# Feature sums of batch 0: from a masked sum on VectorE to a masked operand on GpSimd and small matmuls on TensorE

## The chip, the cores and the metric

The kernel runs on one core of a Trainium2 chip, in one launch. The metric is the time on the device in microseconds (us). A core has engines that run their own queues in order and wait for one another by semaphores: TensorE (PE in the profile, its weight loads PEld), VectorE (DVE), ScalarE (ACT), GpSimd (POOL) and SyncE (SP, which here issues most of the transfers).

## What is computed

The reference has two parts. The first is attention with a sketched polynomial kernel, without softmax: 4 batches, 4 heads, 1088 positions, 32 dimensions a head, r = 8, so 64 features.

```python
def phi(x):
    a = einsum('rd,bhsd->bhsr', S1, x)
    b = einsum('rd,bhsd->bhsr', S2, x)
    return einsum('bhsi,bhsj->bhsij', a, b)      # reshaped to r*r = 64 features
q_p, k_p = phi(q), phi(k)
kv = einsum('bhsf,bhsd->bhfd', k_p, v)
z = sum(k_p, axis=2)                             # feature sums, over all positions
num = einsum('bhsf,bhfd->bhsd', q_p, kv)
den = einsum('bhsf,bhf->bhs', q_p, z)[..., None] + 1e-06
attn = num / den
```

The second part is a gated feed-forward layer over the 4352 tokens, 128 wide: `sigmoid(x @ w_gate) * (x @ w_val) @ w_out` with 1536 inner columns. The weights and S1, S2 arrive as 64-bit floats and are narrowed to 32 bits on the chip; everything is computed in 32-bit floats.

The change concerns `z`, the feature sums, of batch 0 only.

## The kernel before, in words

**The stages.** Most of the time PE does the feed-forward part. Tokens go through it in chunks of 512, and of each chunk in "waves": one wave is a block of 128 inner columns, with matmuls for gate and value (tile `wave`, line 499), a sigmoid on ACT (`sg`, line 507), their product on DVE (`g`, line 538), and later the product with `w_out` (`moeout`, line 382, in the first chunk; `prod`, line 338, in most others). Attention of batches 1 to 3 is threaded in between the waves. Attention of batch 0 has nothing to hide behind: it stands ahead of the first wave, since the wave needs its result `xT`.

**The order of work.** PE, DVE, ACT and POOL run in the order in which the program issues instructions (a manual schedule); each engine's queue is in order. So a waiting instruction holds up what is behind it on its engine. Transfers are issued mainly by SP.

**Batch 0, in the order of the program.** `kT` and `qT` are 32x32 block transposes of k and q on DVE. `kps` (line 628) multiplies k by S1 and S2 and DVE transposes the result into `kab` (line 638), so that positions lie on partitions. `ab` (line 735) makes the two factors of the features of q, `aps` and `bps`; ACT copies the first (`asb`), and DVE multiplies them to `qp` (line 754). `outer` (line 707) multiplies the two factors of k into `kp`, the 64 features; for batch 0 its last step runs on POOL and the others on DVE.

The feature sums of batch 0 are not taken from `kp`. They come from `gram` (line 645): z[i,j] is the sum over positions of a[i] b[j], thus an entry of the product of `kab` with itself. Eighteen small accumulating matmuls (line 651) give it in four partial sums on the four groups of 32 partitions, in bank `acc0`; ACT copies it out as `gs` (line 660). Then:

- `gh` (line 662, POOL): the columns of b, times the mask `e_m` that keeps on each partition the columns of its own head of the pair. 128 partitions by 32 elements.
- `spread_z` (line 674, PE): one matmul with the constant `e_sum` as weights. It sums the four groups and puts z[i,j] for all (i,j) on 128 partitions, every column j of it on every partition.
- `mask_z` (lines 685 and 697, DVE): times the mask `m_col` that keeps the column j of the partition, into `zm`, and a reduction over j, into `zb`. `zb` holds for each head and each half of the partitions one column with the 64 sums.

Then `dn` (line 1012) makes the denominators, `dps` (line 1018), with `zb` as weights; DVE transposes them (`dT`, line 1029). Between, `kv0` (line 834) sums `kp` against v into `kvz`; ACT copies it (`kvd`, line 869), PE transposes it (`ndps`), ACT copies that (`nd`, line 920), PE makes the numerators `nps` (line 1037), and DVE multiplies them by the reciprocals into `xT` (line 1058). Bank `acc0` holds first `gram` and then `kvz`.

**The weights.** `narrow` (line 83) makes 32-bit weights in steps: `cap` on POOL (line 97) and `tail` on ACT (line 101); `head` by two instructions on DVE (lines 105 and 109); `square` on ACT and an integer sum on POOL (line 118); and on DVE the write of `w_sb` (line 127). `narrow_01(part, step)` does this for the first two blocks.

**Fillers.** `warm` issues matmuls of constants, whose results nobody reads. One of them, `warm(512)`, stands on PE between `spread_z` and `dps`:

```python
    for part in range(2):
        narrow_01(part, 0)
    spread_z()
    warm(512)
    for pi in range(2):
        outer(0, pi, 0, 5)
    mult00()
    mult10()
    mask_z()
```

Of the kernel before, what the change touches and what calls it, by code (L numbers as in the profile page):

```python
# [8 lines left out]
F32 = mybir.dt.float32  # L9
# [3 lines left out]
ALU = mybir.AluOpType  # L13
ACTF = mybir.ActivationFunctionType
MUL = ALU.mult

P = 128
# [3 lines left out]
def kernel(  # L21
# [12 lines left out]
    nc = tc.nc  # L34

    B, H, S, D = q.shape
    R = S1.shape[0]
# [14 lines left out]
    const = ctx.enter_context(tc.tile_pool(name="const", bufs=1))  # L52
# [136 lines left out]
    def narrow_01(part, step):  # L189
        if wide:  # L190
            if step == 0:
                i = (slice(0, 2), part) if part < 2 else (2, slice(0, 2))
                narrowing["01", part] = narrow(
                    w_sb[:, i[0], i[1]],
                    w_in[0][:, i[0], i[1]],
                    nc.gpsimd,
                    "acc0" if part else "acc1",
                )
            next(narrowing["01", part])
# [69 lines left out]
    ident = const.tile([P, P], F32, tag="ident")  # L269
    make_identity(nc, ident)  # L270

    e_sum = const.tile([P, 2, R, R], F32, tag="e_sum")
    e_row = const.tile([P, R], F32, tag="e_row")
    e_m = const.tile([P, 2], F32, tag="e_m")
    id_m = ident.rearrange("p (g m x) -> p g m x", g=4, m=2)[:, :, :, :R]

    m_col = const.tile([P, 2, R], F32, tag="m_col")
    nc.gpsimd.memset(m_col, 0.0)
    for c in range(2):
        rows = slice(64 * c, 64 * c + 64)  # L280
        nc.vector.tensor_reduce(
            out=m_col[rows, c],
            in_=ident[rows].rearrange("p (k j) -> p j k", j=R),
            axis=mybir.AxisListType.X,
            op=ALU.add,
        )
    for t, x in (
        (e_row, id_m.rearrange("p g m x -> p x g m")),
        (e_m, id_m.rearrange("p g m x -> p m g x")),
    ):  # L290
        nc.vector.tensor_reduce(out=t, in_=x, axis=mybir.AxisListType.XY, op=ALU.add)
    nc.vector.tensor_copy(
        out=e_sum,
        in_=bass.AP(
            tensor=e_row.tensor,
            offset=e_row.offset,
            ap=[list(e_row.ap[0]), [0, 2], [1, R], [0, R]],
        ),
    )
    eps = const.tile([P, 1], F32, tag="eps")  # L300
    nc.gpsimd.memset(eps, 1e-6)
    zb = const.tile([P, H, 32], F32, tag="zb", name="zb")
# [342 lines left out]
    def gram():  # L645
        t = pso.tile([P, TCH], F32, tag="acc0", name="gram")
        for pi in range(2):
            for j in range(NJK):
                g = 32 * (j % 4)
                x = KAB[0][: 64 if j == 0 else P, pi, j]  # L650
                nc.tensor.matmul(
                    out=t[g : g + 32, 32 * pi : 32 * pi + 32],
                    lhsT=x,
                    rhs=x,
                    start=(j < 4),
                    stop=(j >= NJK - 4),
                    skip_group_check=True,
                )
        gs = const.tile([P, 2, 2, 2, R], F32, tag="gs")
        nc.scalar.copy(out=gs.rearrange("p a m x r -> p (a m x r)"), in_=t[:, :64])  # L660
        gh = const.tile([P, 2, 2, R], F32, tag="gh")
        nc.gpsimd.tensor_tensor(
            out=gh,
            in0=gs[:, :, :, 1],
            in1=bass.AP(
                tensor=e_m.tensor,
                offset=e_m.offset,
                ap=[list(e_m.ap[0]), [0, 2], [1, 2], [0, R]],
            ),
            op=MUL,  # L670
        )

        def spread_z():
            nc.tensor.matmul(
                out=t[:, 64 : 64 + H * R],
                lhsT=e_sum.rearrange("p c i j -> p (c i j)"),
                rhs=gh.rearrange("p a m r -> p (a m r)"),
                start=True,
                stop=True,
            )  # L680

        def mask_z():
            zm = const.tile([P, H, 2, R], F32, tag="zm")
            z0 = t[:, 64 : 64 + H * R]
            nc.vector.tensor_tensor(
                out=zm,
                in0=bass.AP(
                    tensor=z0.tensor, offset=z0.offset, ap=[list(z0.ap[0]), [R, H], [0, 2], [1, R]]
                ),
                in1=bass.AP(  # L690
                    tensor=m_col.tensor,
                    offset=m_col.offset,
                    ap=[list(m_col.ap[0]), [0, H], [R, 2], [1, R]],
                ),
                op=MUL,
            )
            nc.vector.tensor_reduce(
                out=zb[:, :, :2], in_=zm, axis=mybir.AxisListType.X, op=ALU.add
            )

        return spread_z, mask_z


    def outer(b, pi, j0=0, j1=NJK, eng=nc.vector):
        a0 = KAB[b][:, pi, j0:j1]
        ap = [list(a0.ap[0]), [2 * R, 2 * (j1 - j0)]]
        eng.tensor_tensor(  # L707
            out=KP[b][:, pi, j0:j1].rearrange("p j m (i l) -> p (j m) i l", i=R),
            in0=bass.AP(tensor=a0.tensor, offset=a0.offset, ap=ap + [[1, R], [0, R]]),
            in1=bass.AP(tensor=a0.tensor, offset=a0.offset + R, ap=ap + [[0, R], [1, R]]),  # L710
            op=MUL,
        )
# [6 lines left out]
    def ab(a_of=None, b_of=None, pool_b=None):  # L719

        mm = []
        if a_of is not None:
            aps = psm.tile([P, 2, 512], F32, tag="wave", name="aps")
            mm.append((a_of, aps, sa))
        if b_of is not None:
            pool, tag = (ps2, "two") if pool_b is None else pool_b
            bps = pool.tile([P, 2, 512], F32, tag=tag, name="bps")
            mm.append((b_of, bps, sb))
        for c in range(2):
            for m in range(2):  # L730
                for (bb, pr, n), dst, sx in mm:
                    h = 2 * pr + m
                    rows = slice(32 * h, 32 * h + 32)
                    t0, tn = q_chk[n]
                    nc.tensor.matmul(
                        out=dst[64 * c : 64 * c + 64, m, : 32 * tn],
                        lhsT=sx[rows, :],
                        rhs=qT_of[bb][rows, t0 : t0 + tn, c, :],
                        start=True,
                        stop=True,  # L740
                    )
        if a_of is not None:
            w = 32 * q_chk[a_of[2]][1]
            ASB[a_of] = sbA.tile([P, 2, 256], F32, tag="asb", name="asb", bufs=2)
            nc.scalar.copy(out=ASB[a_of][:, :, :w], in_=aps[:, :, :w])
        if b_of is not None:

            def mult():
                bb, pr, n = b_of
                if bb not in QP:  # L750
                    QP[bb] = sbA.tile([P, 2 * H * W1], F32, tag="qp", name="qp")
                t0, tn = q_chk[n]
                w = 32 * tn
                nc.vector.tensor_tensor(
                    out=half(QP[bb], n).rearrange("p (m c) w -> p c m w", m=2)[:, pr],
                    in0=bps[:, :, :w],
                    in1=ASB[b_of][:, :, :w],
                    op=MUL,
                )

            return mult
# [329 lines left out]
    else:  # L1091
        nc.vector.tensor_copy(
            out=s4[:, 1:],
            in_=bass.AP(
                tensor=s4.tensor, offset=s4.offset, ap=[list(s4.ap[0]), [0, 3], [1, D]]
            ),
# [5 lines left out]
        out=st_[:, : 2 * R],  # L1102
        lhsT=s4.rearrange("p g d -> p (g d)"),
        rhs=ident[: 2 * R, : 2 * R],
        is_transpose=True,
        start=True,
        stop=True,
# [5 lines left out]
        out=sk,  # L1113
        in0=bass.AP(
            tensor=st_.tensor, offset=st_.offset, ap=[list(st_.ap[0]), [0, 2], [R, 2], [1, R]]
        ),
        in1=bass.AP(
            tensor=hm.tensor, offset=hm.offset, ap=[list(hm.ap[0]), [R, 2], [0, 2], [1, R]]
        ),
        op=MUL,  # L1120
# [6 lines left out]
    for n, inner in enumerate(([[1, R], [0, R]], [[0, R], [1, R]])):  # L1127
        t = const.tile([P, R, R], F32, tag=f"s{n}", name=f"s{n}")
        s0 = st_[:, n]
        nc.scalar.copy(  # L1130
            out=t, in_=bass.AP(tensor=s0.tensor, offset=s0.offset, ap=[list(s0.ap[0])] + inner)
# [4 lines left out]
    kps(0)  # L1136
    ab((0, 0, 0))
    ab((0, 1, 0))
    spread_z, mask_z = gram()
    mult00 = ab(None, (0, 0, 0))  # L1140
    mult10 = ab(None, (0, 1, 0), (psm, "wave"))
    for pi in range(2):
        outer(0, pi, NJK - 1, NJK, eng=nc.gpsimd)
    for part in range(2):
        narrow_01(part, 0)
    spread_z()
    warm(512)
    for pi in range(2):
        outer(0, pi, 0, 5)
    mult00()  # L1150
    mult10()
    mask_z()


    def rest(turn, rc, dT):
# [201 lines left out]
```

## Time and profile before

| What | us |
|---|---|
| median of 3 runs | 294.46 (293.63 to 294.61) |
| the profiled execution, its own time | 293.7 |
| its span in the profile | 291.9 |
| PE busy | 286.1 |
| DVE busy | 188.4 |
| POOL busy | 162.5 |
| ACT busy | 92.2 |

The span is the time between the first and the last instruction of the profiled execution; its own time has 1.8 us more around that. The granted clock of TensorE in the profile is 1.00 of full speed. "Busy" is time in which an engine executes something; a wait isn't busy. A timeline row gives the start of a group of instructions, its duration, the engine, the line, what is written from what, and in brackets the idle time before it with the instruction that ended it. In the profile a 32-bit matmul shows as two records, each with its weight load.

### The profile page before, as it was taken

To read this page: it belongs to the slowest core of one execution; us is meant where nothing else is said; L and a number is where in the kernel's file an instruction comes from. 1 tells how busy PE (TensorE), PEld (TensorE's weight loads), DVE (VectorE), ACT (ScalarE), POOL (GpSimd) and SP (SyncE) were. 2 spreads that over 40 slices of the span, in tenths; PEclk is the share of its full clock that TensorE was granted. 3 is DMA by queue.
4 is the path that set the end of the run, shared out by engine and by line. 5 is a ranking of instruction groups with operands and counts; after the bars stand their busy time and mean duration, and the time that the engine had idled before them with its cause. 6 is when DMAs were issued, how large, how long until landed. Compare 5 with 4: busy or idle time off the path is not lost.

```text
span 291.9 us, 5783 instructions
## 1 busy us (share of the span) xinstructions
PE 286.1 (98%) x2276; PEld 155.1 (53%) x2276; DVE 188.4 (65%) x320; ACT 92.2 (32%) x168; POOL 162.5 (56%) x221
## 2 busy tenths in 40 slices
PE   8899999999999999999999999999999999999995
PEld 3444433345455455554555555554555555555895
DVE  6998789976837857677556685668336423642482
ACT  3557532322333222323234212423233222322421
POOL 2465554897546558546446597664465655656300
PEclk9999999999999999999999999999999999999999
DMA  7994521584800177406000684102000200020002
GB/s 221 345 347 107 121 94 60 146 164 122 245 1 2 45 181 141 133 25 190 1 0 2 158 149 114 28 2 37 0 2 0 36 2 0 0 37 1 2 4 52
DMA packets 28890, 24.23 MB, mean 83 GB/s; under 512 B 18560, under 2 KB 24064, under 8 KB 28864
## 3 DMA queue, kind: packets, MB, share of 16 engines
q1 hardware_dynamic: 27920, 22.21, 30.7%
q10 hardware_dynamic: 944, 1.66, 1.8%
q8 instruction: 18, 0.29, 0.4%
q14 instruction: 8, 0.07, 0.1%
HBM read 20.60 MB, written 3.26 MB: 82 GB/s over the span
## 4 chain that ended last, share of the span: by engine, by line
PE 85%; DMA 7%; DVE 3%; POOL 2%; issue 1%; SPq 1%; ACT 0%; POOLq 0%
PE wave L499 55%; PE prod L338 22%; DMA w_in<-in_moe_w_val_dram 4%; POOL head L118 2%; PE moeout L406 2%; DMA v<-in_v_dram 2%; DMA kq<-in_q_dram 1%; PE moeout L382 1%; PE kvz L847 1%; DVE w_sb L127 1%; DVE head L109 1%; PE nps L1212 1%; DVE head L105 1%; PE kps L628 1%; PE cqps L774 0%
## 5 line engine op out<-in xcount | busy, mean ns | idle before, releaser
L499 PE MATMUL wave<-xT,w_sb 128*64 128x512 f32 (+3 forms) x820 | 210.7, 566 | 0.1
L499 PEld LDWEIGHTS wave<-xT,w_sb 128*64 128x64 f32 (+1 forms) x820 | 85.5, 140 | 63.3 <-issue 49.3
L538 DVE TENSOR_TENSOR g<-wave,sg 128x512 f32<-128x512 f32 x96 | 65.9, 686 | 76.1 <-ACT sg L507 74.9
L507 ACT ACTIVATE sg<-wave 128x512 f32<-128x512 f32 x102 | 61.0, 598 | 170.5 <-PE wave L499 165.4
L328 POOL TENSOR_TENSOR tsum<-g 128x256 f32<-128x256 f32 x84 | 69.0, 824 | 27.4 <-DVE g L538 27.1
L328 POOL TENSOR_TENSOR tsum<-g,tsum 128x256 f32<-128x256 f32 x42 | 34.2, 815 | 57.9 <-DVE g L538 57.5
L338 PE MATMUL prod<-tsum,ws 128*64 128x256 f32 x252 | 62.8, 381 | 0.0
L338 PEld LDWEIGHTS prod<-tsum,ws 128*64 128x64 f32 x252 | 31.2, 137 | 16.0 <-issue 11.8
L338 PE MATMUL prod<-g,w_sb 128*64 128x256 f32 x168 | 34.9, 383 | 0.0
L328 POOL TENSOR_TENSOR tsum<-tsum,g 128x256 f32<-128x256 f32 x42 | 32.7, 779 | 3.3
L338 PEld LDWEIGHTS prod<-g,w_sb 128*64 128x64 f32 x168 | 15.7, 136 | 18.2 <-issue 15.4
L338 PE MATMUL prod<-tsum,w_sb 128*64 128x256 f32 x84 | 25.3, 383 | 0.0
L338 PE MATMUL prod<-g,ws 128*64 128x256 f32 x84 | 25.0, 379 | 0.0
L118 POOL TENSOR_TENSOR head<-head,tail 128x384 int32<-128x384 int32 (+2 forms) x14 | 13.3, 952 | 17.9 <-DVE head L109 11.5
L338 PEld LDWEIGHTS prod<-g,ws 128*64 128x64 f32 x84 | 11.5, 137 | 3.7
L382 PE MATMUL moeout<-g,w_sb 128*128 128x512 f32 (+1 forms) x28 | 12.6, 607 | 0.3 <-DVE w_sb L127 0.3
L338 PEld LDWEIGHTS prod<-tsum,w_sb 128*64 128x64 f32 x84 | 10.8, 137 | 3.0 <-issue 2.2
L827 DVE TENSOR_TENSOR qp<-qp,bq 128x1152 f32<-128x1152 f32 (+1 forms) x7 | 9.6, 1369 | 3.4 <-DMA bq<-dq 3.4
L707 DVE TENSOR_TENSOR kp<-kab 128x1152 f32<-128x1152 f32 (+2 forms) x10 | 10.9, 1102 | 0.0
L438 DVE TENSOR_TENSOR res<-prod,other 64x512 f32<-64x512 f32 (+1 forms) x14 | 7.6, 544 | 3.1 <-ACT other L432 3.1
L531 DVE TENSOR_TENSOR g<-wave,sg 128x512 f32<-128x512 f32 x6 | 6.5, 1091 | 4.7 <-ACT sg L507 4.7
L473 DVE STREAM_TRANSPOSE o_sb<-res 64x512 f32<-64x512 f32 x14 | 9.5, 687 | 0.0
(121 smaller groups left out, 202.0 us busy)
## 6 DMA issues: line engine op xcount, KB each, us to landing
qp<-dq SPq DMA_DIRECT2D x7, 576.0 KB
bq<-dq SPq DMA_DIRECT2D x14, 288.0 KB
kq<-in_k_dram SPq DMA_DIRECT2D x3, 544.0 KB
kq<-in_q_dram SPq DMA_DIRECT2D x3, 544.0 KB
w_in<-in_moe_w_out_dram SPq DMA_DIRECT2D x6, 256.0 KB
w_in<-in_moe_w_gate_dram SPq DMA_DIRECT2D x5, 256.0 KB
w_in<-in_moe_w_val_dram SPq DMA_DIRECT2D x5, 256.0 KB
out_dram<-o_sb SPq DMA_DIRECT2D x20, 64.0 KB
```

The lines of the kernel that those rows point to most:

```text
L118: nc.gpsimd.tensor_tensor(out=head, in0=head, in1=tail, op=ALU.add)
L328: nc.gpsimd.tensor_tensor(out=t[:, u], in0=in0, in1=in1, op=ALU.subtract)
L338: nc.tensor.matmul(out=out, lhsT=lhsT, rhs=rhs, start=start, stop=stop, skip_group_check=True)
L382: nc.tensor.matmul(out=moe["acc"][d], lhsT=w_sb[:, 2, j, d], rhs=g[:, jj], start=(j == 0), stop=(j == NJ - 1),)
L438: nc.vector.tensor_tensor(out=out, in0=in0, in1=in1, op=op)
L473: nc.vector.transpose(out=o_sb[:64, d].rearrange("p t x -> p (t x)"), in_=r[:, 1 + 2 * d : 3 + 2 * d].rearrange("p u x -> p (u x)"),)
L499: nc.tensor.matmul(out=wv[d, which, jj * tw + o : jj * tw + o + tp], lhsT=w_sb[:, which, j0 + jj, d], rhs=xT[:, t0 + o : t0 + o + tp], sta ...
L507: nc.scalar.activation(out=sg, in_=wv[:, 0], func=ACTF.Sigmoid)
L531: nc.vector.tensor_tensor(out=g.rearrange("p (j u s y) -> p j y u s", j=2, u=2, y=4), in0=wv[:, 1].rearrange("p (j y u s) -> p j y u s", j ...
L538: nc.vector.tensor_tensor(out=g, in0=wv[:, 1], in1=sg, op=MUL)
L707: eng.tensor_tensor(out=KP[b][:, pi, j0:j1].rearrange("p j m (i l) -> p (j m) i l", i=R), in0=bass.AP(tensor=a0.tensor, offset=a0.offset, ...
L827: nc.vector.tensor_tensor(out=q0, in0=q0, in1=half(BQ[b], n), op=MUL)
```

## The change

Constants: `e_sum`, `e_m` and `m_col` go. `e_row` grows to 16 elements for each partition, written twice: which of the two heads and which of the eight columns of a the partition belongs to. New is `e_c`, two pairs of columns: the first is (1, 0), the second (0, 1), on all partitions.

The operand: `gh` on POOL now has all 64 features of 4 heads, 256 elements a partition: b[j] times the mask for i. The sum over the partitions of its column (i, j) is z[i,j].

The matmuls: `spread_z` now has eight, for each head h and half c, with the 64 columns of `gh` as weights and the two columns of `e_c` as the moving operand. Each puts the 64 sums of a head on one half of the partitions, in the column of its half, and 0 in the other. Then ACT copies the 8 columns from the bank to `zb`. `mask_z` goes. In the program `spread_z()` now stands ahead of the first steps of `narrow_01`, so on ACT the copy is ahead of two `tail` instructions, and on the other engines the order of the rest is as before.

```diff
-    e_sum = const.tile([P, 2, R, R], F32, tag="e_sum")
-    e_row = const.tile([P, R], F32, tag="e_row")
-    e_m = const.tile([P, 2], F32, tag="e_m")
-    id_m = ident.rearrange("p (g m x) -> p g m x", g=4, m=2)[:, :, :, :R]
-
-    m_col = const.tile([P, 2, R], F32, tag="m_col")
-    nc.gpsimd.memset(m_col, 0.0)
+    id_m = ident.rearrange("p (g m x) -> p m x g", g=4, m=2)[:, :, :R]
+    e_row = const.tile([P, 2, 2, R], F32, tag="e_row")
+    for a in range(2):
+        nc.vector.tensor_reduce(out=e_row[:, a], in_=id_m, axis=mybir.AxisListType.X, op=ALU.add)
+    e_c = const.tile([P, 2, 2], F32, tag="e_c")
+    nc.vector.memset(e_c, 0.0)
     for c in range(2):
-        rows = slice(64 * c, 64 * c + 64)
-        nc.vector.tensor_reduce(
-            out=m_col[rows, c],
...
-    nc.vector.tensor_copy(
-        out=e_sum,
...
+        nc.vector.memset(e_c[:, c, c : c + 1], 1.0)
...
-        gh = const.tile([P, 2, 2, R], F32, tag="gh")
+        gh = const.tile([P, H, R, R], F32, tag="gh")
+        g0 = gs[:, :, :, 1]
         nc.gpsimd.tensor_tensor(
             out=gh,
-            in0=gs[:, :, :, 1],
+            in0=bass.AP(
+                tensor=g0.tensor, offset=g0.offset, ap=[list(g0.ap[0]), [2 * R, H], [0, R], [1, R]]
+            ),
             in1=bass.AP(
-                tensor=e_m.tensor,
-                offset=e_m.offset,
-                ap=[list(e_m.ap[0]), [0, 2], [1, 2], [0, R]],
+                tensor=e_row.tensor,
+                offset=e_row.offset,
+                ap=[list(e_row.ap[0]), [R, H], [1, R], [0, R]],
             ),
             op=MUL,
         )
 
         def spread_z():
-            nc.tensor.matmul(
-                out=t[:, 64 : 64 + H * R],
-                lhsT=e_sum.rearrange("p c i j -> p (c i j)"),
-                rhs=gh.rearrange("p a m r -> p (a m r)"),
-                start=True,
-                stop=True,
-            )
-
-        def mask_z():
-            zm = const.tile([P, H, 2, R], F32, tag="zm")
...
-            nc.vector.tensor_reduce(
-                out=zb[:, :, :2], in_=zm, axis=mybir.AxisListType.X, op=ALU.add
-            )
-
-        return spread_z, mask_z
+            for h in range(H):
+                for c in range(2):
+                    nc.tensor.matmul(
+                        out=t[64 * c : 64 * c + 64, 64 + 2 * h : 66 + 2 * h],
+                        lhsT=gh[:, h].rearrange("p i j -> p (i j)"),
+                        rhs=e_c[:, c],
+                        start=True,
+                        stop=True,
+                        skip_group_check=True,
+                    )
+            nc.scalar.copy(
+                out=zb[:, :, :2], in_=t[:, 64 : 64 + 2 * H].rearrange("p (h c) -> p h c", c=2)
+            )
+
+        return spread_z
...
     for pi in range(2):
         outer(0, pi, NJK - 1, NJK, eng=nc.gpsimd)
+    spread_z()
     for part in range(2):
         narrow_01(part, 0)
-    spread_z()
     warm(512)
     for pi in range(2):
         outer(0, pi, 0, 5)
     mult00()
     mult10()
-    mask_z()
```

More of the change, by code (lines that the diff above doesn't have):

```diff
@@ L270 @@
     make_identity(nc, ident)
-    e_sum = const.tile([P, 2, R, R], F32, tag="e_sum")
-    e_row = const.tile([P, R], F32, tag="e_row")
-    e_m = const.tile([P, 2], F32, tag="e_m")
-    id_m = ident.rearrange("p (g m x) -> p g m x", g=4, m=2)[:, :, :, :R]
-    m_col = const.tile([P, 2, R], F32, tag="m_col")
-    nc.gpsimd.memset(m_col, 0.0)
-    for c in range(2):
-        rows = slice(64 * c, 64 * c + 64)
-        nc.vector.tensor_reduce(
-            out=m_col[rows, c],
-            in_=ident[rows].rearrange("p (k j) -> p j k", j=R),
-            axis=mybir.AxisListType.X,
-            op=ALU.add,
-        )
[L287 to L291, printed above, removed]
-    nc.vector.tensor_copy(
-        out=e_sum,
[L294 to L298, printed above, removed]
-    )
+    id_m = ident.rearrange("p (g m x) -> p m x g", g=4, m=2)[:, :, :R]
[4 more added lines that the diff above has]
+    nc.vector.memset(e_c, 0.0)
+    for c in range(2):
+        nc.vector.memset(e_c[:, c, c : c + 1], 1.0)
     eps = const.tile([P, 1], F32, tag="eps")
@@ L673, in spread_z @@
         def spread_z():
-            nc.tensor.matmul(
-                out=t[:, 64 : 64 + H * R],
-                lhsT=e_sum.rearrange("p c i j -> p (c i j)"),
-                rhs=gh.rearrange("p a m r -> p (a m r)"),
-                start=True,
-                stop=True,
-            )
-        def mask_z():
-            zm = const.tile([P, H, 2, R], F32, tag="zm")
[L684 to L697, printed above, removed]
-                out=zb[:, :, :2], in_=zm, axis=mybir.AxisListType.X, op=ALU.add
-            )
-        return spread_z, mask_z
+            for h in range(H):
[10 more added lines that the diff above has]
+                out=zb[:, :, :2], in_=t[:, 64 : 64 + 2 * H].rearrange("p (h c) -> p h c", c=2)
+            )
+        return spread_z
     def outer(b, pi, j0=0, j1=NJK, eng=nc.vector):
@@ L1138 @@
     ab((0, 1, 0))
-    spread_z, mask_z = gram()
+    spread_z = gram()
     mult00 = ab(None, (0, 0, 0))
```

## The prediction

> **What bounds the kernel now.** I began with busy time by engine and the table of stretches (columns: stretch, its length, then PE, weight loads (PEld), DVE, ACT, POOL busy, the clock, DMA share, GB/s), since a small edit is worth what its stage makes of it.
>
> ```profile
> PE 286.1 (98%) x2276; PEld 155.1 (53%) x2276; DVE 188.4 (65%) x320; ACT 92.2 (32%) x168; POOL 162.5 (56%) x221
> ```
>
> ```profile
> 9.00:11.00 2.00, 1.58 (x8) 0.68 (x12) 1.97 (x6) 0.76 (x2) 1.63 (x5) 1.00 1.07 379
> 11.00:15.00 4.00, 3.19 (x100) 1.93 (x93) 3.90 (x12) 2.31 (x7) 1.45 (x3) 1.00 1.07 372
> 15.00:19.00 4.00, 3.67 (x13) 2.12 (x14) 3.73 (x9) 2.36 (x6) 2.54 (x4) 1.00 1.06 372
> 19.00:23.20 4.20, 4.20 (x16) 1.54 (x17) 4.03 (x9) 2.55 (x6) 2.07 (x4) 1.00 1.08 272
> 23.20:40.00 16.80, 16.80 (x41) 7.39 (x39) 12.97 (x26) 9.65 (x20) 9.99 (x14) 1.00 0.34 84
> 60.00:285.00 225.00, 225.00 (x1826) 127.28 (x1824) 135.28 (x211) 64.86 (x110) 129.78 (x168) 1.00 0.26 58
> ```
>
> From 23.2 us on PE has no idle time: the end is the moment at which PE gets into that stream plus a fixed amount of matmul work. So whatever shifts the stream's start shifts the end one to one, and nothing else counts. Before it, DVE is the full engine: 1.97 of 2, 3.90 of 4, 3.73 of 4 us. Next the timeline of the stretch that the change edits (start, duration, engine, line, operation; in brackets the idle time before it and who ended it):
>
> ```profile
> 8.68 0.48 POOL L662 TENSOR_TENSOR gh<-gs,e_m 128x32 f32<-128x32 f32 x1 [2.53 <-ACT gs L660]
> 9.21 0.41 PE L674 MATMUL gram<-gh,e_sum 128*128 128x32 f32 x2 [0.28 <-POOL gh L662]
> 9.45 1.11 PE L260 MATMUL warm<-const-float32-1.0 128*128 128x512 f32 x2
> 10.25 0.21 DVE L685 TENSOR_TENSOR zm<-gram,m_col 128x64 f32<-128x64 f32 x1
> 10.50 0.22 DVE L697 TENSOR_REDUCE zb<-zm 128x8 f32<-128x64 f32 x1
> 10.63 1.02 DVE L707 TENSOR_TENSOR kp<-kab 128x384 f32<-128x384 f32 x2
> 10.77 0.64 PE L1018 MATMUL dps<-qp,zb 128*32 128x256 f32 x8 [0.21 <-DVE zb L697]
> 11.57 0.44 DVE L1029 STREAM_TRANSPOSE dT<-dps 128x256 f32<-128x256 f32 x1
> ```
>
> The reader is to see a chain, gh, small matmul, zm, zb, dps, dT, and on two engines what stands in line with it: on PE the filler `warm(512)` lies between the small matmul and dps; on DVE zm and zb lie between the products qp and kp. From dT on DVE runs its queue nearly without a gap up to the write of w_sb at 18.43, for which PE waits with its first moeout at 18.89; only small gaps follow on PE until 23.24. So **the start of dT is the anchor**: a shift of it goes to the end. It stood at two doors: dps ends at 10.77 + 0.64 = 11.41, a consumer follows its PE producer by 0.06 (kvz ends 12.42, its copy starts 12.48), so the data were there at 11.47; DVE came free of kp at 11.57. A delay of dps costs nothing for its first 0.10 us and all above that. (PE's own branch, dps, kvz, nps, has slack too: nps ends 14.16, and xT starts only at 14.38.)
>
> [...] 128x256 takes 724 ns, 128x384 about 1000 where nothing blocks it, so 2.16 ns per element over a fixed 0.17.
>
> ```profile
> L118 POOL TENSOR_TENSOR head<-head,tail 128x256 int32<-128x256 int32 x3 | 2.2, 724 | 3.8 <-ACT kvd L869 2.2 <-DVE head L109 0.9 <-ACT tail L101 0.8
> 39.23 1.35 DVE L827 TENSOR_TENSOR qp<-qp,bq 128x1152 f32<-128x1152 f32 x1
> 39.48 1.96 POOL L118 TENSOR_TENSOR head<-head,tail 128x384 int32<-128x384 int32 x1 [1.13 <-DVE head L109]
> ```
>
> [...] the head of 1.00 takes 1.96 at 39.48, beside qp. The old gh shows it as well: 32 elements should take 0.17 + 32 x 2.16 ns = 0.24, it took 0.48, while kp ran on DVE until 9.05. [...] 189 ns for 128 columns, 110 for 32, so 0.82 ns per column, 53 ns for 64.
>
> **The change part by part.**
> *Setup on DVE.* Out go two m_col reduces (0.38 each), e_row (0.26), e_m (0.21) and e_sum (0.22), and on POOL one memset of 0.11; in come two reduces of 64 elements (about 0.25 each) and three memsets (0.07 each, as hm). DVE ends some 0.7 earlier and then waits for s_in anyway (idle 0.94 before 3.63). Worth 0; if s_in came a microsecond earlier it would gain.
>
> *gh on GpSimd, 128x32 to 128x256.* 224 more elements at 2.16 ns: 0.48 us, end 9.16 to 9.64. Low end 9.41 (no blocking: 8.68 + 0.73), high end 9.9 (half as slow again by the broadcast access; kp on POOL, 128x128 and broadcast likewise, took 400 ns and speaks against it). I take 9.64. Behind gh on POOL stand two kp (0.40 each) and two cap (0.40 each): they move from 9.12-10.62 to about 9.6-11.1. Their readers are kvz's last step and DVE's L105 at 11.94 and 13.21, so there is room, but they now meet DVE's kp[...]; see the third rival.
>
> *The small matmul: 1 of 128x128 by 32 columns becomes 8, of 64 weight columns and 2 moving ones.* The trace counts 2 records for each f32 matmul: 16 instead of 2. Their spacing is not in the trace. Low: 28 ns, if the two column halves overlap as kvz's four column groups do (72 records start within 0.98 us, 14 ns each, for 32 columns). High: 55 ns, one load after another (the old pair, 128 columns each, was 0.11 apart). In between, gram's 36 records of 32 columns start 20.5 ns apart, 0.77 of their load of 26; 0.77 x 53 gives 41 ns, which I take: 0.66 us. PE starts it at 9.64 + 0.06 = 9.70 and is through at 10.36.
>
> *warm(512), unedited,* still comes next on PE: 2 records of 0.43, 0.86 us. Before, it ran in the shadow of zm and zb (9.45 to about 10.31, dps not before 10.77). Now its cover is gone: dps can start at 10.36 + 0.86 = 11.22, that is 0.45 later.
>
> *The copy of zb on ACT instead of zm and zb on DVE.* Last small matmul ends about 10.36 + 0.2 (gram's records take 0.2), the copy starts about 10.62, takes 0.21 (as gs), and zb is there at 10.83 + 0.06, before warm lets PE go: cost 0. ACT is in order, so the two tails behind it (0.76 together at 9.24) wait until 10.83 and end at 11.6; POOL's head wants them at 12.79. The next ACT item, rc, waits for dT and starts at 12.11. Cost 0; cover about 0.5 us.
>
> *DVE without zm and zb:* 10.25 to 10.63, 0.38 us less. kp could then end at 11.2, and dT follow it, if dps were ready. At 11.22 + 0.64 + 0.06 = 11.92 it is not: the gain becomes idle time on DVE.
>
> *Sum:* dT starts at 11.92 instead of 11.57, **+0.35 us** (0.45 less the 0.10). Everything behind moves with it: dT's followers on DVE, the narrowing of the weights, the first wave, the first moeout. The profiled execution took 293.7 (span 291.9, and 1.8 around it), so by its own time 294.05. The three runs' median is 294.46, 0.76 above it, and the forecast stands on that: **294.8 us**. With the low ends of gh and spacing dps starts at 10.77, as before, and the shift is 0 at most; with both high ends 11.7, shift +0.83.
>
> **The rivals.**
> 1. *The freed DVE decides.* PE could be ready sooner: gh at its low end, 9.41, and the small matmuls nearly free behind one another (14 ns as kvz's, 0.22 us). Then dps starts at 10.55, kp ends at 11.2, and dT follows at 11.25, 0.32 earlier: 294.1. For it: DVE is full from 9 to 19 us. Against it: it takes both low ends, and warm's 0.86 stays.
> 2. *Slower: weight loads do not overlap at all.* [...] at 0.11 each, 16 take 1.76, dps starts at 12.3, the shift is 1.45: 295.9. It passes 0.3% (0.88 us) once dps is 0.98 late, which means a spacing over 74 ns. [...] Against it: gram and kvz, far below.
> 3. [...] POOL's kp and cap now alternate with DVE's two kp of 0.51 (10.3 to 11.3). Worst: one kp and one cap of 0.40 ahead of DVE's two, kp ends at about 11.8 to 12.1, and dT at 12.1 rather than 11.92: 295.0. In the other order POOL waits, and nothing is lost.
> 4. *Nothing arrives at the end,* since PE's stream regains 0.35 later: 294.5. Only small gaps are left (19.94 of 20 us busy from 40 to 60), so little speaks for it.
>
> **How the numbers follow.** 0.3% of 294.46 is 0.88 us, about what a measurement of this kernel can tell from no change. The main case has 0.58 (0.48 within 0.3%, 0.10 slower, for both high ends and the scatter of about half a microsecond that the three runs show). Rival 1 has 0.16 (0.11 within, 0.05 faster), rival 2 0.12 (0.11 slower, 0.01 within), rivals 3 and 4 together 0.14 (0.07 within, 0.04 faster and 0.03 slower, for later stages that fall into step differently). Sums: faster 0.09, same 0.67, slower 0.24. The range runs from rival 1 less some scatter, 293.9, to just short of rival 2, 295.7.
>
> **What would show it right or wrong.** In the profile after: gh of about 0.96 us on POOL, ending at 9.64; 16 records on PE within 0.7 us; warm right behind; dps released by PE's own queue and not by zb, at 11.2; DVE idle before dT for some tenths; first moeout at about 19.2; the later stages as before. The forecast fails if dps starts before 10.8 or after 11.8, if dT is released by something other than dps, or if the shift at the first moeout is not the shift at the end.

## The result: a little slower, by more than its direct cost

The first comparison, 10 executions each: 295.63 us median after (294.61 to 297.34) against 294.40 before (293.63 to 296.09), ratio 1.0045 [1.0027, 1.0063]. The forecast was 294.8 us and no measurable change; the measured time lies at the upper edge of its range, and the change of 1.2 us is clear of no change by its interval. The changed kernel was measured twice more, beside experiments: 1.0012 [0.9995, 1.0030] and 1.0005 [0.9988, 1.0023]. The three differ by more than their intervals allow, which the experiments had to explain; weighted, they give about 1.002, 0.6 us. Ratios leave out the few executions that lie over 1.5% above the fastest; the counts of executions below keep them.

The profiled execution after took 295.2 us (span 293.3). First its engines and three of the stretches shown for before (stretch, length, PE, PEld, DVE, ACT, POOL busy, clock, DMA share, GB/s):

```profile
PE 286.8 (98%) x2290; PEld 155.4 (53%) x2290; DVE 187.8 (64%) x318; ACT 92.3 (31%) x169; POOL 162.0 (55%) x220
```

```profile
9.00:11.00 2.00, 1.35 (x18) 0.84 (x18) 2.00 (x4) 0.61 (x3) 2.00 (x5) 1.00 1.07 377
11.00:15.00 4.00, 3.26 (x100) 1.93 (x99) 3.71 (x11) 2.13 (x7) 1.41 (x3) 1.00 1.07 374
60.00:285.00 225.00, 224.57 (x1814) 126.12 (x1812) 134.09 (x211) 64.84 (x110) 128.98 (x169) 1.00 0.25 59
```

From 9 to 11 us POOL is full and PE has less to do (1.35 of 2, it was 1.58); the last row has lost 0.43 us of PE's stream, which was whole before. The edited stretch in the timeline after:

```profile
8.73 0.86 POOL L643 TENSOR_TENSOR gh<-gs,e_row 128x256 f32<-128x256 f32 x1 [2.44 <-ACT gs L640]
9.65 0.63 PE L659 MATMUL gram<-e_c,gh 128*64 128x2 f32 x16 [0.66 <-POOL gh L643]
10.22 1.13 PE L260 MATMUL warm<-const-float32-1.0 128*128 128x512 f32 x2
10.30 1.08 POOL L97 TENSOR_SCALAR cap<-w_in 128x256 f32<-128x256 f32 x2
10.31 1.49 DVE L677 TENSOR_TENSOR kp<-kab 128x384 f32<-128x384 f32 x2
10.39 0.17 ACT L667 COPY zb<-gram 128x8 f32<-128x8 f32 x1 [1.73 <-POOL kp L677]
11.27 0.64 PE L988 MATMUL dps<-qp,zb 128*32 128x256 f32 x8
11.98 0.45 DVE L999 STREAM_TRANSPOSE dT<-dps 128x256 f32<-128x256 f32 x1 [0.18 <-PE dps L988]
```

The reader is to see zb ready at 10.56, dps starting only when the filler lets PE go, and DVE idle for 0.18 us ahead of dT until dps is done. Execution to execution, the stretch starts at different times: the first transpose `kab` stood at 6.77 us before, at 6.83 here, and at 7.36 in the run without the filler below. So the stretch is best measured from kab:

| from the start of kab, us | dps | dT | first wave |
|---|---|---|---|
| before | 4.00 | 4.80 | 8.08 |
| after | 4.44 | 5.15 | 8.44 |

dT is 0.35 later. The first moeout comes at 19.32 instead of 18.89, so that shift arrives. But at the end the two profiled spans differ by 1.4. Comparing the start of the sigmoids `sg` one by one, the lag is 0.42 at the first, 0.37 from the twelfth (47 us) to the 22nd (74 us), and 1.46 from the 23rd (79 us) to the end. In between, PE waits within the attention of batch 1, at `denj`, matmuls for its denominators. The timeline of PE there, before and then after:

```profile
74.08 0.50 PE L976 MATMUL denj<-b,zw 64*32 64x160 f32 x16
```

```profile
74.70 0.48 PE L946 MATMUL denj<-b,zw 64*32 64x160 f32 x8 [0.18 <-DMA b<-dq]
75.42 0.48 PE L946 MATMUL denj<-b,zw 64*32 64x160 f32 x8 [0.25 <-DMA b<-dq]
```

Before, denj ran through; after, it stood twice until transfers from `dq` landed, a buffer in memory through which the factors of q pass on their way to other partitions.

### The profile page after: what moved, and what is told of

It is laid out like the page before. It is cut to its first block, busy times and chain, and to the rows that moved or that the text cites. A ratio compares the mean times of both kernels' runs of the same rounds, so it can differ in the third digit from the quotient of the medians.

```text
span 293.3 us, 5810 instructions
## 1 busy us (share of the span) xinstructions
PE 286.8 (98%) x2290; PEld 155.4 (53%) x2290; DVE 187.8 (64%) x318; ACT 92.3 (31%) x169; POOL 162.0 (55%) x220
## 4 chain that ended last, share of the span: by engine, by line
PE 77%; DMA 16%; DVE 2%; SPq 2%; POOL 1%; issue 1%; ACT 0%; POOLq 0%
PE wave L479 49%; PE prod L318 20%; DMA bq<-dq 7%; DMA v<-in_v_dram 3%; DMA w_in<-in_moe_w_out_dram 2%; PE moeout L386 2%; DMA w_in<-in_moe_w_gate_dram 2%; POOL head L118 1%; PE moeout L362 1%; DMA dq<-cq 1%; PE nps L1181 1%; SPq L769 1%; PE kvz L817 1%; PE kps L608 1%; DVE w_sb L127 1%
## 5 line engine op out<-in xcount | busy, mean ns | idle before, releaser
L308 POOL TENSOR_TENSOR tsum<-g 128x256 f32<-128x256 f32 x84 | 68.1, 812 | 29.9 <-DVE g L518 29.7
```

The source lines that it names most:

```text
L308: nc.gpsimd.tensor_tensor(out=t[:, u], in0=in0, in1=in1, op=ALU.subtract)
```

## The experiments

Twelve kernels ran, in three groups. Theory A: the filler lost its cover, dps is late, and the rest follows. Theory C, formed after the first group: TensorE does too little from 9 to 10.2 us, and in some executions its granted clock falls. An execution whose mean granted clock lies under 0.996 is said to have lapsed; all others have 0.998 or more.

**The filler away, after the change.**

```diff
     spread_z()
     ...
-    warm(512)
```

> The changed kernel without the filler warm(512) between the small matmuls and dps. Theory A (the filler lost its cover, and all else follows from the late start): dps is then released by the copy of zb, at about 10.65 instead of 11.27; dT is held by DVE's kp, which ends at about 11.73, so it starts at 11.75 instead of 11.98, the first wave 0.2 to 0.5 earlier than after (14.8 to 15.05), and the late loss at batch 1 shrinks as well: 294.3 to 294.8. Theory B (the filler is irrelevant, the eight small matmuls and gh cost by themselves): dps still at 11.0 or later, and the time stays at about 295.5.

Measured: 1.0006 [0.9989, 1.0024]. From kab, dps came at 3.78 and dT at 4.93: 0.22 of the 0.35 came back, as theory A says, and dT was then held by kp on DVE, which took 1.53. The first wave itself stood at 15.57, later than expected, because kab started 0.6 later than before in that execution (7.36); from kab it was 8.21. Theory B falls. The late loss didn't shrink as theory A had it: it was 0.76 between the twelfth and the 23rd sigmoid. Four of the 14 executions lapsed. (The ratio is not the quotient of the medians; these, 295.06 and 294.39, lie 0.67 us apart, so the time says less here than the profile.)

**Only the lateness, on the kernel before.**

```diff
     spread_z()
-    warm(512)
+    warm(512, 512)
```

> The kernel before, with warm(512, 512) in place of warm(512): nothing but a later dps, about 11.2, as late as in the changed kernel. Theory A (only the lateness counts): dT at 11.9, first wave at 15.2 to 15.3, and in the end the whole of the change's loss, about +1.2 us, 295.6, of which 0.4 at the first wave and the rest at batch 1's attention. Rival 1 (the lateness is worth only itself): +0.4, 294.8. Rival 2 (gh on GpSimd, the copy on ACT or the small matmuls do further harm of their own): less than +0.4.

Measured: 1.0017 [0.9998, 1.0037], about +0.5 us; from kab, dps 4.58, dT 5.29, first wave 8.58. Lateness is worth about itself, as rival 1 says; theory A's 1.2 us lies just outside the interval. No execution of 14 had a clock below 0.999. The profiled one lost 0.75 at batch 1, although it has the old sums.

**Without the stores of the first chunk, after and before.**

```diff
     slot(lambda: parts(1), 1)
-    moe["store"]()
```

> The changed kernel without the four stores of the first token chunk (its output rows are left out): three of them stand on SP just as ACT sends cq of batch 1 to dq. Theory A (the second loss is the transfer of dq that shares the DMA engines with these stores): dq lands within 1.7 us of its issue instead of 3.0, denj does not wait on PE, and the lag against the kernel before stays at +0.4 to the end: about 294.5, and +0.4 against the same edit of the kernel before. Rival (the second loss comes from something else, the stores are innocent): still about 295.6, or +1.2 against its partner.

> The kernel before without the four stores of the first token chunk, the partner of the run above. Theory A: 293.7 to 294.4, since dq then lands at least as early as in the profile before (2.3 us after its issue) and nothing else changes. Rival: no difference from the kernel before.

Measured: 1.0014 [0.9993, 1.0034] and 0.9994 [0.9981, 1.0008]; their quotient is 1.0020, some 0.6 us, with an interval of about 0.0025 either way, so neither 0.4 nor 1.2 us is excluded. The first read of dq was released on SP 2.1 us after ACT had issued the transfer to it; in the changed kernel with the stores this took 3.0, but in the kernel before, with the same stores, 2.3. So it is not shown that the stores slow dq. The loss at batch 1 was still 0.58 without them: they are not its cause, or not alone, and this part of theory A falls. Three of 14 executions of the changed kernel without stores had clocks of 0.992 to 0.994, which led, with the four of the run without the filler, to theory C.

**Fillers and the clock.** Four kernels side by side: a filler added ahead of the small matmuls; the filler moved there; the kernel before without its filler; the changed kernel again.

```diff
+    warm(256)
     spread_z()
     for part in range(2):
         narrow_01(part, 0)
     warm(512)          # stays in the first, goes in the second
```

> The changed kernel with one more filler, warm(256), ahead of the eight small matmuls, in the time in which PE waits for gh (8.94 to 9.65); the one behind them stays. Theory C (beside the late start, the changed kernel lets TensorE do so little from 9 to 10.2 us that in about a quarter of its runs the granted clock is taken back for some microseconds: 9 of 38 runs of the three kernels with the change had a mean clock of 0.992 to 0.994, none of 87 with the old sums): the small matmuls start at the same time, the stretch to dT is as in the changed kernel (5.15 us from the first transpose kab to dT), and no run has a clock under 0.997; the time is 0.3 to 0.6 below that of the changed kernel in this call, about 294.9. Rival (the clock has nothing to do with it): the same share of runs at 0.993, the same time.

> The changed kernel with the filler moved: warm(256) ahead of the small matmuls, none between them and dps. Theory A and C together: dps is released by the copy of zb, 3.8 us after the start of kab (before 4.00, after 4.44), dT is held by DVE's kp and comes 4.93 us after kab (before 4.80, after 5.15), no clock under 0.997, and the time lies 0.1 to 0.3 above the kernel before, about 294.6. Rival: as slow as the changed kernel, since the small matmuls and gh are the cost.

> The kernel before without its filler warm(512) between the small matmul and dps. Its chain does not contain the filler (dps is released by zb), so dps and dT stay at 4.00 and 4.80 us after kab. Theory C: with PE idle from about 9.6 to 10.8, some runs (one in ten or more) show a mean clock of 0.992 to 0.994, as the changed kernel's do, and those are 1 us or more longer. Rival: no such runs, median as before.

> The changed kernel itself, once more, to stand beside the three others on the same chip. Theory A and C: +0.3 to +0.45% against the kernel before, a fifth to a third of its runs at a clock of 0.992 to 0.994. Rival (the first measurement had bad luck): within 0.2% of the kernel before, and no such runs.

| kernel | ratio to before | executions with a clock under 0.996 |
|---|---|---|
| filler added ahead | 1.0015 [1.0000, 1.0031] | 0 of 22 |
| filler moved ahead | 1.0003 [0.9988, 1.0017] | 2 of 22 |
| before, no filler | 1.0014 [0.9996, 1.0032] | 4 of 14 |
| changed, again | 1.0012 [0.9995, 1.0030] | 2 of 22 |

(The count of 9 of 38 in the expectation should have been 10, and of the 87 with the old sums one had lapsed too.) Three expectations of theory C failed here. The kernel with the filler added ahead had no lapse, but was not faster than the changed kernel (1.0015 against 1.0012; a gain of 0.3 us would be lost in these intervals). The one with the filler moved ahead lapsed twice, where no lapse was expected. And the changed kernel itself lapsed in 2 of 22, not in a fifth or more, and lost 0.12% rather than 0.3: in its time it lies nearer to the rival. The timeline with the filler moved shows what the change can do at best:

```profile
8.89 0.70 PE L260 MATMUL warm<-const-float32-1.0 128*128 128x256 f32 x2
9.62 0.63 PE L659 MATMUL gram<-e_c,gh 128*64 128x2 f32 x16
10.28 1.51 DVE L677 TENSOR_TENSOR kp<-kab 128x384 f32<-128x384 f32 x2
10.58 0.64 PE L988 MATMUL dps<-qp,zb 128*32 128x256 f32 x8 [0.32 <-ACT zb L667]
11.72 0.43 DVE L999 STREAM_TRANSPOSE dT<-dps 128x256 f32<-128x256 f32 x1
```

dps is now released by the copy of zb, but dT waits for DVE: kp took 1.51 instead of 1.02, while POOL ran cap beside it (10.26 to 11.37, 1.11 instead of 0.77); POOL's own kp had just ended, at 10.29. So the 0.38 us that DVE gave up went into a longer kp. From kab: dps 3.78, dT 4.92. The added filler costs nothing: dT 5.15 as before it. In the kernel before without its filler dT stays at 4.79, as expected, and lapses appear; the four lapsed executions lie 0.95 us above the others by their medians.

**A gap made on purpose.** To catch a lapse in a profile, gh was made eight times over in the kernel before, without and with fillers in the gap; beside them the changed kernel with its whole filler ahead, and unedited.

```diff
+        for _ in range(8):
             nc.gpsimd.tensor_tensor(out=gh, ...)
 ...
+    warm(512, 512)     # in the second only
     spread_z()
-    warm(512)
```

> The kernel before with gh made eight times over on GpSimd (the same result each time) and without the filler behind the small matmul: PE has nearly nothing to do from 8.9 to 11.7 us. The chain is later by what gh costs, dT about 5.8 us after kab instead of 4.80, so +1.0 us by lateness alone, 295.5. Theory C (too little work on TensorE lets the granted clock fall): a third or more of the runs, more than the 4 of 14 of the kernel before without its filler, have a mean clock of 0.994 or less, and are 1 to 3 us longer than the others. Rival: no more lapses than there.

> The same with fillers, warm(512, 512), in the gap, ahead of the small matmul, where PE waits for gh: the chain is as late (dT about 5.8 us after kab). Theory C: no run with a clock under 0.996, and a time of +1.0 us over the kernel before. Rival: as many lapses as its partner without fillers, and the same time.

> The changed kernel with its filler warm(512) moved from behind the small matmuls to ahead of them. They start some 0.15 later than with a free PE, dps about 3.95 us after kab (before 4.00), dT is held by DVE's kp at 4.93 (before 4.80, after 5.15). Theory A and C: no clock under 0.996, within 0.1% of the kernel before. Rival: +0.3%, as slow as the changed kernel was at first.

> The changed kernel a third time; the first two measurements gave 1.0045 and 1.0012 of the kernel before. Theory A and C: dT 5.15 us after kab, a steady +0.35 us, and a tenth to a third of the runs with a lapsed clock: a ratio of 1.001 to 1.003. Rival 1 (the first measurement is the true one): 1.004 or more. Rival 2 (the late start does not arrive at the end): 1.000.

Measured: with the gap 298.17 us (1.0126 [1.0094, 1.0159]), every one of 6 executions at a clock of 0.994 or less; with the gap filled 296.15 (1.0058 [1.0041, 1.0075]), none of 11. dT came at 6.79 and 6.75 from kab, not at 5.8: eight gh took longer than I had counted (they ran from 9.0 to about 11.7 with the gap). The lateness is the same in both (dps at 5.65 and 5.64 from kab), so some 2 us of the first is clock. The stretches of PE (stretch, length, PE busy, clock, DMA share, GB/s) with the gap, and with the gap filled:

```profile
9.00:11.00 2.00, 0.26 (x15) 1.00 1.07 369
11.00:13.00 2.00, 0.67 (x6) 0.94 1.10 382
13.00:15.00 2.00, 2.00 (x64) 0.50 1.03 363
15.00:17.00 2.00, 1.26 (x37) 0.71 1.07 376
```

```profile
9.00:11.00 2.00, 1.79 (x4) 1.00 1.07 378
11.00:13.00 2.00, 1.06 (x26) 1.00 1.06 365
13.00:15.00 2.00, 1.56 (x73) 1.00 1.07 373
```

The clock was 0.50 from 13 to 15 us, and 0.94 and 0.71 in the 2 us ahead and behind. If all of this is one stretch at 0.50, an estimate from the three means, it went from about 12.8 to 16.2 us, just where dps and kvz run. Their rows in PE's timeline, with the gap and then filled:

```profile
12.74 1.08 PE L1019 MATMUL dps<-qp,zb 128*32 128x256 f32 x8 [0.57 <-DVE zb L698]
13.59 2.15 PE L835 MATMUL kvz<-kp,v 128*32 128x64 f32 x72
```

```profile
12.35 0.64 PE L1019 MATMUL dps<-qp,zb 128*32 128x256 f32 x8 [0.57 <-DVE zb L698]
12.80 1.42 PE L835 MATMUL kvz<-kp,v 128*32 128x64 f32 x72
```

dps takes 1.08 instead of 0.64, kvz 2.15 instead of 1.42. The first wave comes 10.97 us after kab with the gap, 10.02 with the gap filled. Estimated from this trace, one such stretch, 3.4 us at 0.50, costs up to 1.7 us of PE's work and takes 0.006 off the mean clock of a span of 295.9 us. The six executions had 0.994, 0.988 or 0.983, which by this estimate would fit one, two or three stretches; only one, at 0.994, was profiled. When the clock falls and for how long, in general, no run here shows.

The changed kernel with its whole filler ahead: 1.0006 [0.9991, 1.0021], no lapse in 22, dps at 4.11 (3.95 expected), dT at 4.92, all near what was expected. Unedited: 1.0005 [0.9988, 1.0023], 2 lapses in 14, dT at 5.15. The dT and the share of lapses are as expected, the ratio is below the expected 1.001 to 1.003, and its interval excludes the 1.004 of the first measurement.

## Why the prediction was right and where it was wrong

**The steps of the sum hold.** gh ended at 9.59 (9.64 forecast; it took 0.86, of which DVE's kp ran beside it for 0.37, less than the 0.96 priced), the 16 records and the filler's start lie 0.57 apart, 35 ns a record (41 taken), the copy of zb was done in time, dps came at 11.27 and dT at 11.98 (11.22 and 11.92, in an execution whose kab was 0.06 late). From kab the shift of dT is 0.35, the number forecast, in four of the five profiles that have the new sums and the filler in its place (dT at 5.15), and 0.41 in one. Rival 2 falls: 35 ns is far from 74. Rival 3 was right that kp would be longer beside POOL: it took 1.49 beside cap (1.02 before) and ended at 11.80 instead of the 11.2 of the sum. That one of the two engines waits for the other there was the author's estimate: cap was longer as well, 1.08 instead of 0.77. And the rival was wrong in its effect: dps was later still. So DVE's freed time went mostly into the longer kp, and only 0.18 us became the idle time that the sum had expected.

**The step that failed is "nothing else counts".** The prediction took the end for PE's start plus a fixed amount of work, at a clock of 1.00, because the one profile shows both. It put a loss of clock, and any wait behind 23.2 us, at nothing. The direct shift was right, but the end moved by more: of the signs that it named for its failure, the last came true, 0.43 us at the first moeout and 1.4 at the end. Two things are not fixed.

First, the clock. Of the 46 executions of the changed kernel 7 lapsed; of the 157 of the kernel before whose clocks are known, 2. (The profiled one after has a clock of 1.00; no lapsed execution of the changed kernel was profiled, so where in it the clock fell is not seen.) In each of its three comparisons the lapsed ones lay above the median of the others, by 1.8, 2.7 and 1.3 us: on average 1.9 us in 15% of executions, 0.3 us. The others lie above the kernel before by 0.84, 0.30 and 0.18 us, weighted by their number 0.36, which is close to the direct shift, though the three scatter widely about it. Together 0.65 us, the 1.002 of the three comparisons. The first had 3 lapses in 10, some 0.5 us; with the direct 0.35 that leaves 0.4 to 0.5 us of its difference unexplained, which did not return in the other two. So its size is in part bad luck, and by the other two alone the forecast of no measurable change would have held. The likely reason for more lapses is that PE waits 0.66 us for gh and then does matmuls of two columns until 10.2; the prediction had this stretch ("PE starts it at 9.70", "0.66 us"), but priced it as lateness alone. That low work of PE brings lapses is shown by the gap and its fill (6 of 6 against 0 of 11); that it is this for the changed kernel is less certain. The one with a filler added ahead had 0 of 22 against 7 of 46, which chance alone would give about once in 18; the three with a filler ahead had 2 of 66 together, the two other edits of the changed kernel (no filler, no stores) 7 of 28.

Second, batch 1. The loss between the twelfth and the 23rd sigmoid, against the profile of before, was 0.6 to 1.1 us in ten of the thirteen later profiles, and none in the rest:

| | profiles with it | without |
|---|---|---|
| old sums | delayed 0.75; no filler 0.77; gap 0.93; filled 0.60 | no stores |
| new sums | 1.09, 0.58, 0.58 (unedited); no filler 0.76; no stores 0.58; whole filler ahead 0.66 | filler added; filler moved |

All of it arises between the 22nd and the 23rd sigmoid, but not at one wait. In five of the ten profiles PE's denj waits for copies from dq, as after; in two more (no stores, whole filler ahead) denj takes 0.94 and 1.01 in place of 0.50. In the other three (filled, and both repeats of the changed kernel) denj runs through, and PE waits 0.33 to 0.35 at `nps` for DVE's `g`. There DVE's queue was late: its product `qp` waited for the transfers and then took longer (1.88 us in the row below, 1.36 before). The rows of before, then of the changed kernel measured again:

```profile
72.33 1.36 DVE L827 TENSOR_TENSOR qp<-qp,bq 128x1152 f32<-128x1152 f32 x1 [1.61 <-DMA bq<-dq]
```

```profile
73.48 1.88 DVE L797 TENSOR_TENSOR qp<-qp,bq 128x1152 f32<-128x1152 f32 x1 [1.69 <-DMA a<-dq]
76.03 1.16 PE L1181 MATMUL nps<-qp,nd 64*32 64x512 f32 x32 [0.35 <-DVE g L518]
```

What the ten have in common is that qp stands 1.69 to 2.72 us for transfers from dq; in the four without the loss it is 0.90 to 1.61. Late transfers are thus the likely source, which no experiment shows.

The loss comes with the old sums and with the new ones (four of six profiles and six of eight, too few to say that the change leaves its frequency alone), so the change is not needed for it. The profile of before, at 293.7 us against a median of 294.4, was one of those that escape it, and the profile after had the largest: most of the 1.4 us between the two is this. The forecast added the difference between its own time and the median to both kernels, which was right; taking PE's stream for whole, as that one profile shows it, was not. What decides for an execution whether the transfers are late stays open: the stores were tried and don't explain it alone, and of the other traffic nothing was tried.

**The chances.** 0.24 for slower by over 0.3% came from slow loads, the high ends and late stages; the clock was not among the cases. On the pooled ratio the change is about 0.2% slower, at the limit of what can be told from no change.

**A better version.** With the filler moved ahead the change loses its lateness (1.0003, 1.0006), but nothing beat the kernel before: dT is then held by DVE's kp, which took 1.51 beside POOL's cap (1.02 before).

## What to carry to other kernels

A filler on an engine in order is free only as long as the wait behind it is longer than it (before, dps waited until 10.77 for zb, behind the filler; after, zb was there at 10.56 and the filler held dps until 11.27); when an edit moves the wait ahead of it, the filler should move too. An edit that makes TensorE wait has to be priced for two things, the lateness (here dT 0.35 us later) and the clock (lapsed in 6 of 6 executions with the gap, 0 of 11 with it filled); look at the granted clock of every execution, not of the profiled one alone. And one profile shows one execution: a stream that just fits there may have no slack in the median.

## What was not expected of the hardware

- The clock seems to fall with a pause much shorter than the 2.50 us of the gap. In the kernel before without its filler, PE's longest wait in that stretch is 1.15 us in the profiled execution (which did not lapse, at 0.998), and 4 of 14 executions lapsed, at 0.988 to 0.994:

```profile
10.94 0.64 PE L1018 MATMUL dps<-qp,zb 128*32 128x256 f32 x8 [1.15 <-DVE zb L697]
```

- Weight loads of 64 columns on alternating column halves followed one another every 35 ns, below the 53 ns that the prediction estimates for one such load from the records of 128 and 32 columns (189 and 110 ns), and below the 138 ns of its own record. So the loads overlapped (16 of them in 0.55 us):

```profile
9.65 0.55 PEld L659 LDWEIGHTS gram<-e_c,gh 128*64 128x64 f32 x16 [1.12 <-POOL gh L643]
```

- A GpSimd operation with one input (cap) went with a longer product on DVE: kp took 1.49 beside POOL's cap and 1.02 before, when POOL was idle, and cap took 1.08 beside kp and 0.77 before, when it ran ahead of kp:

```profile
9.85 0.77 POOL L97 TENSOR_SCALAR cap<-w_in 128x256 f32<-128x256 f32 x2
```
